# Attention and a Fourier mixer on one core: the query maximum subtracted on GpSimd, the exponential table loaded behind each root, and an empty step ahead of the transform's blocks

## The chip, the core and the metric

One core of a Trainium2 chip runs the whole kernel. Its engines work side by side, each in its own order of instructions: TensorE (PE: matmuls; PEld: its weight loads), VectorE (DVE), ScalarE (ACT), GpSimd (POOL); SyncE (SP) issues most transfers. The metric is the device time of one execution in microseconds, the median of several.

## The reference, cut to what matters

```python
# efficient attention, 8 batches, 8 heads, 576 tokens, head width 64
q_s = np.exp(q - max over the head's 64);   q_s = q_s / (sum over the 64 + 1e-9)
k_s = np.exp(k - max over the 576 tokens);  k_s = k_s / (sum over tokens + 1e-9)
kv  = einsum('bhsd,bhse->bhde', k_s, v)
x   = einsum('bhsd,bhde->bhse', q_s, kv)      # then heads side by side: (8, 576, 512)
# Fourier mixer and feed-forward
u  = x + real(fft(fft(x, tokens), columns))
un = (u - mean(u)) / sqrt(var(u) + 1e-6)
out = u + relu(un @ w_ch1) @ w_ch2            # 512 -> 2048 -> 512
```

All of it is in fp32.

## The kernel before

The rows are worked on in nine groups: the own tokens of the eight batches (four tiles of 128 rows each) and one group of tokens that the batches share. Group by group, TensorE does the up-projection and the down-projection (for the first group plainly, for the others by Strassen's seven products of halves). Into the up-projection of one group the attention of the next batch is mixed, step by step, and into the down-projection that batch's transform (the Fourier mixer) and its norm. A scheduler then orders the instructions of each engine by its own estimates, so a changed instruction can move others.

The query tiles. An even batch has five (four of its own and one of shared rows), an odd one four:

```python
def q_exp(self, it):
    q = self.live[it][0]
    heads = q.rearrange("p (h d) -> p h d", h=H)                       # 128 x 8 x 64
    V.reduce_max(m[:], heads, axis=AX.X, negate=True)                  # L519, DVE
    for h in range(H):
        nc.scalar.activation(heads[:, h, :], heads[:, h, :], ACT.Exp, bias=m[:, h:h + 1])   # L521, ACT
    V.reduce_sum(rec[:], heads, axis=AX.X)                             # L523
    V.tensor_scalar(out=rec[:], in0=rec[:], scalar1=ATT_EPS, ...)      # L524
    V.reciprocal(rec[:], rec[:])                                       # L525
    V.tensor_tensor(out=heads, in0=heads, in1=spread(rec), op=ALU.mult)  # L526
# then: four PE transposes (L532), ACT copy (L539; L545 for the shared rows), product with kv (L564)
```

The key tiles: maximum on DVE (L455), exponential with a bias on ACT (L457), PE transposes (L467), ACT copy (L468), product with v (L484), and the result scaled into place by DVE (`kvr`, L487).

The transform: four steps of folds on DVE and POOL (L603 to L625), then five blocks of PE products (L655, L658):

```python
    folds = [tokens_folded, columns_folded, by_frequency, columns_again] if b else [at_first]
    return folds + [lambda k=k: block(k) for k in (2, 3, 0, 1, 4)]
```

The norm of a group:

```python
def scales(s):
    nc.scalar.activation(std[:, s], mv[:, s, 1], ACT.Sqrt, bias=self.eps[:, 0:1])   # L730, ACT
    V.reciprocal(std[:, s], std[:, s])                                               # L731, DVE
    V.scalar_tensor_tensor(out=mv[:, s, 0], ...)                                     # L732, DVE
def normal(i):       # groups after the first
    nc.scalar.activation(un[:, 0:D], x, ACT.Identity, bias=..., scale=...)           # L744, ACT
def turn(i):         # four PE transposes (L750), one ACT copy (L754)
```

After it, DVE and POOL combine the transposed rows for Strassen (L348 to L351), and the next up-projection's matmuls (L850) start. In the up-projection, ACT takes the Relu (L857, L862) and POOL makes the sums of its results that the down-projection (L886) needs, four instructions at a time (`a_side`, L341 to L344). In the first group's down-projection (L789), the weights' Strassen sums are made and stored as well (L341 to L351 on DVE and POOL).

The exponential and the root are in different tables of ScalarE. A table load is put in front of an activation whose function is not in the loaded one.

Of the kernel before, what the change touches and what calls it, by code (L numbers as in the profile page):

```python
# [40 lines left out]
F32 = mybir.dt.float32  # L41
# [5 lines left out]
P = 128  # L47
# [75 lines left out]
class _Block:  # L123
# [389 lines left out]
    def q_exp(self, it):  # L513
        nc, V = self.nc, self.nc.vector
        q = self.live[it][0]
        heads = q.rearrange("p (h d) -> p h d", h=H)
        spread = lambda t: t[:].unsqueeze(2).to_broadcast([P, H, DH])
        m = self.small.tile([P, H], F32, tag="qm", name="qm", bufs=3)
        V.reduce_max(m[:], heads, axis=AX.X, negate=True)  # L519
        for h in range(H):  # L520
            nc.scalar.activation(heads[:, h, :], heads[:, h, :], ACT.Exp, bias=m[:, h:h + 1])  # L521
        rec = self.small.tile([P, H], F32, tag="qrec", name="qrec", bufs=3)
        V.reduce_sum(rec[:], heads, axis=AX.X)  # L523
        V.tensor_scalar(out=rec[:], in0=rec[:], scalar1=ATT_EPS, scalar2=None, op0=ALU.add)  # L524
        V.reciprocal(rec[:], rec[:])  # L525
        V.tensor_tensor(out=heads, in0=heads, in1=spread(rec), op=ALU.mult)  # L526
# [63 lines left out]
    def transform(self, b):  # L590


        nc, V, G = self.nc, self.nc.vector, self.nc.gpsimd
        Z = self.work.tile([P, KT, HD], F32, tag="Z", name="Z", bufs=1)
        self.Z[b] = Z
        x = {(c, u): self.xpart(b, c, u) for c in range(2) for u in range(2)}
        eo = {}

        def tokens_folded(some=range(4)):
            for i in some:  # L600
                e, op = ((V if b == 0 else G), ALU.add) if i < 2 else (V, ALU.subtract)
                eo[i] = self.halves()
                e.tensor_tensor(out=eo[i][:, 0:D], in0=x[i % 2, 0], in1=x[i % 2, 1], op=op)  # L603

        def columns_folded(some=range(4)):
            for i in some:
                e, op = ((V if b == 0 else G), ALU.add) if i < 2 else (V, ALU.subtract)
                t = eo[i]
                e.tensor_tensor(out=t[:, 1:HD], in0=t[:, 1:HD], in1=t[:, D - 1:HD:-1], op=op)
                if b == 0:  # L610
                    self.warm(t[:, 0:HD], 2)

        def by_frequency(some=range(4)):

            for i in some:
                e, op = ((G, ALU.add), (G, ALU.subtract), (V, ALU.add), (V, ALU.subtract))[i]
                one, two = eo[i // 2 * 2], eo[i // 2 * 2 + 1]
                (V if b == 0 else e).tensor_tensor(out=eo[i][:, NN:], in0=one[:, 0:NN], in1=two[:, 0:NN], op=op)

        def columns_again(some=(2, 3, 0, 1)):  # L620

            for i in some:
                t, y = eo[i], eo[i][:, NN:]
                V.tensor_tensor(out=t[:, 0:QD], in0=y[:, 0:QD], in1=y[:, HD:QD:-1], op=ALU.subtract)
                V.tensor_tensor(out=y[:, 0:QD], in0=y[:, 0:QD], in1=y[:, HD:QD:-1], op=ALU.add)  # L625

        def at_first():

            for some in ((2, 3), (0, 1)):
                for f in (tokens_folded, columns_folded, by_frequency, columns_again):  # L630
                    f(some)

            t = self.small.tile([P, 1], F32, tag="root", name="root", bufs=1)
            V.tensor_scalar(out=t[:], in0=eo[1][:, NN:NN + 1], scalar1=0.0, scalar2=None, op0=ALU.mult)
            nc.scalar.activation(t[:], t[:], ACT.Sqrt)
            self.wait_for(eo[1][:, NN:], [self.raws[i] for i in range(4)])

        def block(k):


            g = self.live["g", b]
            sines = k in (2, 3)
            own = slice(*{0: (NN, NN + QD), 4: (NN + QD, NN + QD + 1), 1: (0, QD), 2: (NN + 1, NN + QD + 1),
                          3: (1, QD)}[k])
            tail = slice(*{0: (0, QD), 4: (QD, QD + 1), 1: (NN, NN + QD), 2: (1, QD + 1), 3: (NN + 1, NN + QD)}[k])
            n = own.stop - own.start
            if k == KT:

                own, tail = slice(own.start, own.start + P), slice(tail.start, tail.start + P)
            full = self.acc((own.stop - own.start, 512))  # L650
            pz = full[0:n]
            f = sines * NM
            for odd, at, size in ((1, 0, MO), (0, MO, ME)):
                t = eo[3 - odd if sines else odd]
                nc.tensor.matmul(full[:, at:at + size], lhsT=t[:, own], rhs=self.ft[:, f + at:f + at + size], start=at == 0,  # L655
                                 stop=False, skip_group_check=True)
            f += 2 * NM
            nc.tensor.matmul(full[:, 0:NM], lhsT=g[:, tail], rhs=self.ft[:, f:f + NM], start=False, stop=True,  # L658
                             skip_group_check=True)
            z, zt = (self.Zr[0:1], self.ZTr[0:1]) if k == KT else (Z[0:n, k, :], self.ZT[0:n, k, :])  # L660
            nc.scalar.copy(paired(z), interleaved(pz[:, NT - 1:NT - 1 + 2 * ME])[:, 0:P, :])

            at = W * (b % 2)
            nc.scalar.mul(paired(zt[:, at:at + Q]), interleaved(pz[:, 0:2 * MO])[:, 0:NT - 1, ::-1],
                          -1.0 if sines else 1.0)
            nc.scalar.copy(paired(zt[:, at + Q:at + W]), interleaved(pz[:, 0:2 * ME])[:, NT - 2::-1, ::-1])

        folds = [tokens_folded, columns_folded, by_frequency, columns_again] if b else [at_first]
        return folds + [lambda k=k: block(k) for k in (2, 3, 0, 1, 4)]

    def second(self, z, zr, add):

# [43 lines left out]
    def norm(self, g):  # L716

        nc, V = self.nc, self.nc.vector
        mv = self.small.tile([P, 4, 2], F32, tag="mv", name="mv", bufs=2)
        std = self.small.tile([P, 4], F32, tag="std", name="std", bufs=2)  # L720
        unT = self.work.tile([P, 7, 2, HD], F32, tag="unT", name="unT", bufs=1)
        uns = {}

        def stats(i):
            st = self.small.tile([P, 6], F32, tag="st", name="st", bufs=2)
            V.bn_stats(st[:], self.xpart(g, i % 2, i // 2))
            V.bn_aggr(mv[:, i, :], st[:])

        def scales(s):
            nc.scalar.activation(std[:, s], mv[:, s, 1], ACT.Sqrt, bias=self.eps[:, 0:1])  # L730
            V.reciprocal(std[:, s], std[:, s])  # L731
            V.scalar_tensor_tensor(out=mv[:, s, 0], in0=mv[:, s, 0], scalar=-1.0, in1=std[:, s], op0=ALU.mult,  # L732
                                   op1=ALU.mult)

        def normal(i):
            un = self.halves()
            x = self.xpart(g, i % 2, i // 2)
            if g == 0:
                V.tensor_scalar(out=un[:, 0:D], in0=x, scalar1=std[:, i:i + 1], scalar2=mv[:, i, 0:1], op0=ALU.mult,
                                op1=ALU.add)  # L740
                if i == 1:
                    self.wait_for(un, [self.raws[i] for i in range(4, 11)])
            else:
                nc.scalar.activation(un[:, 0:D], x, ACT.Identity, bias=mv[:, i, 0:1], scale=std[:, i:i + 1])  # L744
            uns[i] = un

        def turn(i):
            pt = self.turned()
            for k in range(KT):
                nc.tensor.transpose(pt[:, k, :], uns[i][:, k * P:(k + 1) * P], self.ident[:])  # L750

            c, u = i % 2, i // 2
            cols = slice(c * P, (c + 1) * P)
            nc.scalar.copy(unT[:, u:u + 3:2, :, cols], pt[:].rearrange("p (a k) t -> p a k t", a=2))  # L754

        def all_stats():

            for some in ((0, 2), (1, 3)) if g == 0 else (range(4),):
                for i in some:
                    stats(i)  # L760
                scales(slice(some[0], 4, some[1] - some[0]))

        def combine():
            if g > 0:
                self.b_side(lambda i: unT[:, i], lambda i: unT[:, i], V, nc.gpsimd, V)

        return unT, [all_stats] + pipelined((0, 2, 1, 3), [normal, turn]) + [combine]
# [177 lines left out]
def kernel(ctx: ExitStack, tc: tile.TileContext, q, kT, v, w1, w2, ft,  # L945
# [4 lines left out]
    def front(b, loads=None):  # L950

        first = blk.attention(b, loads)
        steps = late(lambda: blk.transform(b), 9 if b else 6)
        mixes = [lambda c=c: blk.mix_own(b, c) for c in range(2)]
        if b % 2:

# [136 lines left out]
```

## Time and profile before

| | before |
|---|---|
| time, median of 3 (lowest to highest) | 1143.22 us (1142.0 to 1143.67) |
| span of the profiled execution | 1140.2 us |
| granted TensorE clock, mean | 0.996 |
| table loads in front of k's exponentials (L457) | 7, of 1283 ns each |
| table loads in front of the norm's root (L730) | 7, of 1283 ns each |
| query exponentials (L521) | 288, mean 337 ns |

The page gives each engine's busy time as a share of the span. The view by stretch splits that by time: for each stretch its length, the busy time of PE, PEld, DVE, ACT and POOL with the number of instructions in brackets, the granted clock, the share of DMA time and the GB/s. A timeline line gives start, duration, engine, source line, operation and shapes; in square brackets stands how long the engine had been idle before it, and what ended that.

### The profile page before, as it was taken

How to read it: one execution, taken by the hardware profiler on the slowest of the kernel's cores; microseconds unless marked ns; L12 is line 12 of the kernel's file. 1: busy time of each engine (PE TensorE's matmuls, PEld its weight loads, DVE VectorE, ACT ScalarE, POOL GpSimd, SP SyncE). 2: the span in 40 equal slices, each digit the busy share in tenths (PEclk: the TensorE clock that was granted, in tenths of full speed). 3: DMA queues.
4: the chain of work that ended last, by engine and by line, in shares of the span. 5: the costliest groups of instructions: out<-in, count | busy, mean ns of one | idle time of the engine just before them, and what ended most of it. 6: DMA issues, size and time to landing. Idle time of an engine off the chain costs nothing.

```text
span 1140.2 us, 14639 instructions
## 1 busy us (share of the span) xinstructions
PE 1098.6 (96%) x5472; PEld 919.1 (81%) x5472; DVE 543.4 (48%) x1110; ACT 397.7 (35%) x956; POOL 332.5 (29%) x302
## 2 busy tenths in 40 slices
PE   5899999989999999999999999999999999999997
PEld 4644556878888988888889888888889888888886
DVE  6785756488324833384435643683344352203201
ACT  6495423274124513371226322641233142201200
POOL 2075541245012600324024402260034213302320
PEclk9999999999999999999999999999999999999999
DMA  9377784463346534554356436543453344444451
GB/s 310 120 258 243 258 279 148 149 213 140 122 150 206 202 111 143 183 195 154 124 176 213 148 113 190 195 172 107 143 191 148 114 163 148 185 139 154 150 185 55
DMA packets 92549, 193.79 MB, mean 170 GB/s; under 512 B 23088, under 2 KB 59696, under 8 KB 85312
## 3 DMA queue, kind: packets, MB, share of 16 engines
q1 hardware_dynamic: 90680, 191.82, 49.5%
q10 hardware_dynamic: 1800, 1.05, 0.3%
q8 instruction: 43, 0.70, 0.2%
q14 instruction: 26, 0.21, 0.1%
HBM read 168.72 MB, written 28.31 MB: 173 GB/s over the span
## 4 chain that ended last, share of the span: by engine, by line
PE 79%; DVE 11%; ACT 4%; DMA 2%; issue 2%; POOL 1%; SPq 0%; ACTq 0%; POOLq 0%; DVEq 0%
PE bb L850 14%; PE bb L886 13%; PE bc L886 10%; PE bc L850 9%; PE ba L850 9%; PE ba L886 8%; PE acc L484 3%; PE acc L564 2%; PE bc L789 2%; PE acc L655 2%; PE acc L658 2%; PE acc L678 1%; PE tr L750 1%; PE tr L532 1%; PE tr L467 1%
## 5 line engine op out<-in xcount | busy, mean ns | idle before, releaser
L850 PE MATMUL bb<-unT,big 128*128 128x256 f32 x768 | 187.9, 381 | 0.3 <-DVE u L822 0.3
L886 PE MATMUL bb<-big 128*128 128x256 f32 x768 | 172.8, 379 | 0.0
L850 PEld LDWEIGHTS bb<-unT,big 128*128 128x128 f32 x768 | 142.8, 190 | 23.8 <-DVE u L818 3.4
L886 PEld LDWEIGHTS bb<-big 128*128 128x128 f32 x768 | 145.1, 190 | 20.1
L341 POOL TENSOR_TENSOR big<-big 128x512 f32<-128x512 f32 (+1 forms) x38 | 45.1, 1187 | 309.5 <-ACT big L862 305.6
L850 PE MATMUL bc<-unT,big 128*128 128x256 f32 x512 | 125.3, 379 | 0.0
L850 PE MATMUL ba<-unT,big 128*128 128x256 f32 x512 | 124.3, 379 | 0.0
L862 ACT ACTIVATE big<-big 128x512 f32<-128x512 f32 x96 | 60.2, 628 | 171.3 <-DVE big L861 171.0
L886 PE MATMUL bc<-big 128*128 128x256 f32 x512 | 116.5, 379 | 0.5 <-DVE x L903 0.5
L886 PE MATMUL ba<-big 128*128 128x256 f32 x512 | 114.1, 379 | 0.0
L886 PEld LDWEIGHTS bc<-big 128*128 128x128 f32 x512 | 95.9, 190 | 14.1 <-DVE x L903 0.9
L886 PEld LDWEIGHTS ba<-big 128*128 128x128 f32 x512 | 95.9, 190 | 12.3
L850 PEld LDWEIGHTS bc<-unT,big 128*128 128x128 f32 x512 | 95.5, 190 | 12.5
L850 PEld LDWEIGHTS ba<-unT,big 128*128 128x128 f32 x512 | 95.0, 190 | 11.7
L822 DVE TENSOR_TENSOR u<-bb,s 128x512 f32<-128x512 f32 x40 | 27.6, 689 | 134.8 <-PE bb L886 79.1
L521 ACT ACTIVATE q<-q,qm 128x64 f32<-128x64 f32 x240 | 61.5, 337 | 10.2 <-DVE qm L519 9.4
L349 POOL TENSOR_TENSOR unT<-unT 128x512 f32<-128x512 f32 x8 | 14.2, 1773 | 172.9 <-DVE unT L348 172.9
L818 DVE TENSOR_TENSOR u<-bb,s 128x512 f32<-128x512 f32 x40 | 27.6, 690 | 76.8 <-PE bb L850 38.1
L898 POOL TENSOR_TENSOR x<-x,u 128x512 f32<-128x512 f32 x14 | 17.7, 1267 | 148.2 <-DVE u L822 118.0
L861 DVE TENSOR_TENSOR big<-bc,u 128x512 f32<-128x512 f32 x64 | 44.1, 688 | 26.1 <-PE bc L850 25.3
L814 ACT COPY s<-ba 128x512 f32<-128x512 f32 x40 | 23.4, 584 | 89.4 <-PE ba L886 45.5
L754 ACT COPY unT<-tr 128x512 f32<-128x512 f32 x36 | 20.6, 585 | 86.5 <-PE tr L750 86.0
(221 smaller groups left out, 1656.7 us busy)
## 6 DMA issues: line engine op xcount, KB each, us to landing
big<-w1s SPq DMA_DIRECT2D x64, 896.0 KB
big<-w2s SPq DMA_DIRECT2D x56, 1024.0 KB
big<-in_w_dram SPq DMA_DIRECT2D x21, 512.0 KB
k<-in_kT_dram SPq DMA_DIRECT2D x26, 288.0 KB
q<-in_q_dram SPq DMA_DIRECT2D x27, 256.0 KB
v<-in_v_dram SPq DMA_DIRECT2D x26, 256.0 KB
words<-in_w_dram SPq DMA_DIRECT2D x11, 512.0 KB
w2s<-big SPq DMA_DIRECT2D x8, 512.0 KB
```

The costliest lines, as they stand in the source:

```text
L341: e1.tensor_tensor(out=to(4), in0=at(2), in1=at(3), op=ALU.add)
L484: nc.tensor.matmul(pk, lhsT=ks[:, c, :], rhs=v[:, c, :], start=(c == 0), stop=(c == NC - 1))
L521: nc.scalar.activation(heads[:, h, :], heads[:, h, :], ACT.Exp, bias=m[:, h:h + 1])
L564: nc.tensor.matmul(px[:, r * P:(r + 1) * P], lhsT=qT[:, r, :], rhs=self.kvr[b % 2][:, r, :], start=True, stop=True)
L655: nc.tensor.matmul(full[:, at:at + size], lhsT=t[:, own], rhs=self.ft[:, f + at:f + at + size], start=at == 0, stop=False, skip_group_chec ...
L814: nc.scalar.copy(temp("s1"), box["ba"][:])
L818: V.tensor_tensor(out=temp("u2"), in0=box["bb"][:], in1=box["s1"][:], op=ALU.add)
L822: V.tensor_tensor(out=temp("u3"), in0=box["bb"][:], in1=box["s1"][:], op=ALU.add)
L850: nc.tensor.matmul(bank()[:, i, :], lhsT=w[:, WA_AT[m], k * P:(k + 1) * P], rhs=unT[:, B_AT[m], k, :], start=first and i == 0 and k == 0, ...
L861: V.tensor_tensor(out=hp(i), in0=bank[:], in1=u[:], op=ALU.add)
L862: nc.scalar.activation(hp(i), hp(i), ACT.Relu)
L886: nc.tensor.matmul(bank()[:, i, :], lhsT=h[p][:, A_AT[m], i * P:(i + 1) * P], rhs=w[:, p, :], start=first and i == 0 and p == 0, stop=p == ...
```

## The change

Three things. The maximum of a query head is no longer given to eight exponentials as their bias: POOL subtracts it from the whole tile, and one exponential of 128 x 512 follows. For all norms but the first group's, a tiny exponential stands right behind the root, so that the table of exponentials is loaded there and not later in front of a key tile. From batch 2 on, the transform has an empty step between its folds and its blocks, so that the blocks are mixed one step later into the down-projection.

```diff
@@ q_exp
-        V.reduce_max(m[:], heads, axis=AX.X, negate=True)
-        for h in range(H):
-            nc.scalar.activation(heads[:, h, :], heads[:, h, :], ACT.Exp, bias=m[:, h:h + 1])
+        V.reduce_max(m[:], heads, axis=AX.X)
+        nc.gpsimd.tensor_tensor(out=heads, in0=heads, in1=spread(m), op=ALU.subtract)
+        nc.scalar.activation(q, q, ACT.Exp)
@@ transform
-        return folds + [lambda k=k: block(k) for k in (2, 3, 0, 1, 4)]
+        return folds + [lambda: None] * (b > 1) + [lambda k=k: block(k) for k in (2, 3, 0, 1, 4)]
@@ norm, scales
             nc.scalar.activation(std[:, s], mv[:, s, 1], ACT.Sqrt, bias=self.eps[:, 0:1])
+            if g > 0:
+                t = self.small.tile([P, 1], F32, tag="root", name="root", bufs=1)
+                nc.scalar.activation(t[:], std[:, 0:1], ACT.Exp)
             V.reciprocal(std[:, s], std[:, s])
@@ front: number of the transform's steps
-        steps = late(lambda: blk.transform(b), 9 if b else 6)
+        steps = late(lambda: blk.transform(b), (6, 9, 10)[min(b, 2)])
```

## The prediction

> **What bounds the kernel now.** I read the page's first two parts first, then the busy time by stretch, then the timeline around every place where TensorE (PE) stood still.
>
> ```profile
> span 1140.2 us, 14639 instructions
> PE 1098.6 (96%) x5472; PEld 919.1 (81%) x5472; DVE 543.4 (48%) x1110; ACT 397.7 (35%) x956; POOL 332.5 (29%) x302
> ```
>
> PE is the bound and its work does not change, so the change is worth only the PE idle time that it removes or adds. The busy time by stretch says where that idle is (first number after the length: PE busy):
>
> ```profile
> 0.00:60.00 60.00, 40.52 (x234) 33.75 (x234) 43.12 (x125) 35.11 (x100) 10.28 (x30) 0.97 0.65 205
> 120.00:150.00 30.00, 25.82 (x116) 15.77 (x115) 24.54 (x60) 15.60 (x49) 12.96 (x17) 1.00 0.82 296
> 150.00:220.00 70.00, 70.00 (x306) 47.19 (x305) 38.26 (x81) 20.70 (x47) 22.98 (x23) 1.00 0.56 179
> 220.00:260.00 40.00, 36.26 (x204) 30.74 (x203) 28.96 (x61) 26.41 (x74) 14.02 (x12) 1.00 0.58 199
> 260.00:460.00 200.00, 200.00 (x1054) 177.72 (x1054) 96.10 (x192) 64.54 (x165) 49.08 (x39) 1.00 0.44 152
> 460.00:500.00 40.00, 38.71 (x217) 33.62 (x216) 22.03 (x50) 21.96 (x55) 15.38 (x14) 1.00 0.66 225
> 700.00:760.00 60.00, 58.42 (x328) 51.16 (x327) 36.88 (x72) 31.97 (x82) 21.30 (x19) 1.00 0.58 199
> 1120.00:1140.20 20.20, 12.07 (x55) 9.97 (x53) 1.70 (x4) 0.00 (x0) 0.00 (x0) 0.88 0.18 51
> ```
>
> Start 19.5, batch 1's attention 4.2, batch 2's 3.7, batches 4 and 6 1.3 and 1.6, tail 8.1: 38 of the 41.6 us. Between, PE hardly rests. The tail is the last store, which the change leaves alone. So outside the start some 11 us can be had at all. A 128x256 matmul shows 379 ns but the next starts 216 ns later (32 in 6.91 us), so a stall is 0.16 us longer than the idle shown behind one. A steady stall looks like this, in batch 2's attention:
>
> ```profile
> 229.16 0.74 DVE L455 TENSOR_REDUCE km<-k 128x1 f32<-128x576 f32 x1
> 229.93 1.28 ACT L457 ACT_TABLE_LOAD   x1
> 231.22 0.78 ACT L457 ACTIVATE k<-k,km 128x576 f32<-128x576 f32 x1
> 232.14 0.66 PE L467 MATMUL tr<-ident,k 128*128 128x128 f32 x4 [1.47 <-ACT k L457]
> 236.79 4.88 ACT L521 ACTIVATE q<-q,qm 128x64 f32<-128x64 f32 x20
> 254.11 0.66 PE L532 MATMUL tr<-ident,q 128*128 128x128 f32 x4 [1.32 <-DVE q L526]
> ```
>
> The maximum of k is ready at 229.90, but the table load stands in front of its exponential, and PE waits 1.63 us in all. Further on ACT (ScalarE) is full of eights of small exponentials, and PE waits four more times for transposes of q: 0.77, 0.47 and 1.48 us.
>
> [...] Here the load takes 1283 ns, but the exponential starts 10 ns behind it: a switch is worth 1.28 us here[...]. [...] The trace has 337 ns for a 128x64 exponential with bias, eight of them in 2.02 us; a 128x512 Relu of SBUF without one takes 628. [...] The trace: 1.27 us for 128x512 undisturbed, against 0.69 on DVE (VectorE). [...] DVE's normalising product of q (L526) takes 0.69 at the median and up to 1.60, and its small addition (L524) 1.28 instead of 0.17 at 744.9, both while POOL works.
>
> **The change part by part.**
>
> *The query exponentials.* 36 tiles (five for an even batch, four for an odd one) each lose 2.02 us of ACT and gain 0.63 of ACT (as the 128x512 Relu) and 1.27 of POOL. ACT sheds 36 x 1.39 = 50 us, POOL gains 46 and goes from 29% to 33%. For one tile the chain hardly moves: 1.27 + 0.63 + about 0.1 of hand-over is 2.00 against 2.02. Only where tiles queue on ACT is anything gained.
> - Start: in 16.05 to 27.28 us four tiles' exponentials hold ACT for 8.2 us, mixed with copies. The POOL order puts three subtractions ahead of the folds of the shared rows and two behind them. ACT's order puts two exponentials ahead of the copy of the transposed shared rows, so that copy and the folds come about 1.1 us later. The last tile's exponential then ends near 25.3 instead of 27.28, after which DVE (three quarters busy) passes on most of it: PE's wait at 31.38 ends about 1.5 us earlier. **+1.5**.
> - Batch 1 (120 to 150 us): PE's 2.86 us wait at 123 is for data of k and stays. The one at 145.8 (1.65 us) is for DVE's eviction of kv, which stands in DVE's queue behind the sum of the fourth tile. That tile's subtraction now comes on POOL behind additions for the Strassen weights that wait for a DMA until 142.3. Subtraction to about 145.1, exponential to 145.8, against 144.3 now: the wait grows. **-1.0**.
> - Batch 2: the four-Strassen-sums of the up-projection (L341 to L344, 5.2 us) hold POOL until 235.2; the first maximum is there at 236.6, so the first tile is neither helped nor hurt, the later ones gain 1 to 2 us. Its table load also goes (below): 1.63 would fall by 1.28, but in the new PE order that transpose stands four matmuls (0.86 us) earlier, which eats most of it. Of the 4.3 us of listed waits I give back **+2.0**.
>
> *The table behind the root.* Loads go from 16 to 19: the seven in front of k's exponentials become one (batch 1, whose norm has no preload), each of eight norms gets one, and a second root load comes between the last two norms. Stalls that vanish: batches 4 and 6, at 476.9 and 720.5, each 1.20 us for the transpose and 0.35 for the product behind it; PE's order there has the transpose where it was. 2 x 1.55 = **+3.1**. The price is in the norm: the tiny exponential reads std, and the reciprocal overwrites std in place, so VectorE must wait for load and exponential, 1.28 + 0.20 us, before the normalised rows can be made. For groups 2 to 7 the transposes of the rows come 1.2 to 4 us behind the rows now, or are moved 1.7 to 3 us later, so this is hidden. For norm(1) at 191 to 201 us it is not: rows end 199.56, last transpose 200.18, next projection 200.62. **-1.5**.
>
> *The empty step.* For batches 2 on, most blocks of the transform come eight matmuls (1.73 us) later on PE, and so do most transposes of the norm in even groups. What waited there: 0.32 at 769.6 and 0.72 at 888.5 for the folds, 0.55 at 801.8 for the normalised rows. **+1.5**. The projection of the next group then follows the last transpose at once, as it does already at 446.7 without a stall (1.73 us of the first product go ahead of the one that needs the combined rows).
>
> Sum: 1.5 - 1.0 + 2.0 + 3.1 - 1.5 + 1.5 = 5.6 us, so 1143.2 - 5.6 = **1137.6 us**.
>
> **The rivals.**
> 1. *POOL becomes the wait.* [...] a subtraction behind four Strassen sums can be 5 us late, and a subtraction waiting for its maximum holds up sums that the down-projection needs. For it: 36 more POOL instructions[...]. Against: POOL now idles 306 us in front of L341, and in even batches the subtractions stand between finished groups of sums. It would cost 1 to 2 us in each of batches 2 to 6: 1143 to 1148.
> 2. *The gain at the start is larger.* If ACT alone held the start, 5 tiles x 1.39 = 7 us less work could become 4 to 5 us: 1133. Against: DVE does 2.4 us of work for each tile and is 79% busy from 20 to 40 us, and the folds of the shared rows get later.
> 3. *All is hidden:* the scheduler re-places transposes earlier wherever its estimate of ACT falls, and every place is again a near miss. Then 1142 to 1144.
> 4. *The norm's longer chain shows in every group*, 1 us x 6: it would cancel the table loads, 1142.
>
> **Range and chances.** The only large idle is at the start, and no step above moves more than 5 us, so 2% (23 us) is out of reach in both directions. The terms are each uncertain by 1 to 2 us, and eight new placements of PE work are not to be foreseen: 1131.5 to 1144.5. I give faster by over 2% 0.01, within 2% 0.98, slower by over 2% 0.01.
>
> **What would show it.** Right: ACT near 353 us busy (397.7 - 50 + 3 loads of 1.28 + 8 x 0.2), POOL near 378; no table load in front of k's exponentials after batch 1; no PE wait above 0.5 us near 470 to 480 and 715 to 725; a wait of 1 to 2 us near 201; first 60 us with 1 to 2 us less idle. Wrong: PE transposes of q waiting for POOL by way of ACT and DVE (rival 1), or more than 3 us won before 60 us (rival 2), or waits of PE for normalised rows in later groups (rival 4).

## The result and the profile after

| | before | after |
|---|---|---|
| time, median of 4 (lowest to highest) | 1142.61 us (1140.6 to 1143.67) | 1156.49 us (1154.42 to 1158.38) |
| ratio to before, 95% interval | | 1.0123 [1.01, 1.0146] |
| span of the profiled execution | 1140.2 us | 1155.1 us |
| granted TensorE clock, mean | 0.996 | 0.988 |

The change costs 1.2%, some 14 us, where the prediction had a gain of 5.6. First the page's head of the kernel after:

```profile
span 1155.1 us, 14453 instructions
PE 1106.3 (96%) x5472; PEld 925.6 (80%) x5472; DVE 545.3 (47%) x1110; ACT 357.6 (31%) x715; POOL 371.4 (32%) x338
```

The work moved as foreseen: ACT from 397.7 to 357.6 (predicted 353), POOL from 332.5 to 371.4 (predicted 378). PE has the same 5472 matmuls, yet is 7.7 us longer busy: part of them ran at a lower clock. So the loss is in PE's waits and in its clock. The busy time by stretch of the kernel after (length, then PE, PEld, DVE, ACT, POOL busy, clock, DMA share, GB/s):

```profile
0.00:60.00 60.00, 39.98 (x219) 34.08 (x220) 40.82 (x113) 26.65 (x61) 14.43 (x34) 0.91 0.65 204
...
260.00:460.00 200.00, 196.61 (x1037) 174.47 (x1036) 97.74 (x199) 60.07 (x128) 62.52 (x51) 0.99 0.45 156
460.00:500.00 40.00, 39.38 (x214) 34.35 (x213) 17.77 (x38) 12.11 (x22) 13.21 (x12) 1.00 0.55 181
500.00:700.00 200.00, 197.50 (x1054) 175.80 (x1053) 102.46 (x205) 63.43 (x132) 64.35 (x53) 1.00 0.47 160
```

From 460 to 500 there is a little less idle, as predicted. But 260 to 460, where PE did not rest before (200.00), now has 3.4 us of idle, 500 to 700 has 2.5, and the clock of the first 60 us fell from 0.97 to 0.91. As the kernels drift apart, a fixed window compares different work. So I cut the two traces at PE's own marks: the start of the first matmul of each up- and each down-projection. In us, worked out from the starts in the traces:

| from mark to mark | before | after | difference | predicted (minus is a gain) |
|---|---|---|---|---|
| start, to the first up-projection | 61.0 | 64.7 | +3.7 | -1.5 |
| first up-projection | 56.2 | 57.0 | +0.8 | 0 |
| first down-projection (batch 1's attention, norm(1)) | 83.4 | 88.3 | +4.9 | +1.0 + 1.5 |
| up-projection with batch 2 | 67.9 | 71.5 | +3.6 | -2.0 |
| up-projections with batches 4 and 6 | 131.3 | 135.0 | +3.8 | -3.1 |
| up-projections with batches 3, 5, 7 | 187.1 | 187.8 | +0.7 | 0 |
| down-projections with batches 2 to 7 (transforms, norms) | 348.9 | 346.8 | -2.2 | -1.5 |
| the rest, to PE's last matmul | 196.8 | 196.8 | 0 | 0 |

The loss lies in the rows in which queries are worked on; the down-projections with the transforms got faster. The waits of PE in the kernel after, by what they waited for (us in total, times, longest), show a releaser that was 0.3 us in all before:

```profile
PE bb L855 <- DVE u L823: 5.0, 2, 2.5
PE bb L855 <- DVE u L827: 2.6, 1, 2.6
```

These are three waits of an up-projection's matmul for `u`, DVE's eviction of an earlier product. The timeline of the second of them:

```profile
508.26 0.68 DVE L519 TENSOR_REDUCE qm<-q 128x8 f32<-128x512 f32 x1
...
508.95 1.71 POOL L341 TENSOR_TENSOR big<-big 128x512 f32<-128x512 f32 x1 [4.29 <-DVE qm L519]
...
510.61 1.04 POOL L520 TENSOR_TENSOR q<-q,qm 128x512 f32<-128x512 f32 x1
...
511.69 0.63 ACT L521 ACTIVATE q<-q 128x512 f32<-128x512 f32 x1 [1.85 <-POOL q L520]
...
512.35 0.69 DVE L523 TENSOR_REDUCE qrec<-q 128x8 f32<-128x512 f32 x1 [2.75 <-ACT q L521]
...
513.07 1.08 DVE L524 TENSOR_SCALAR qrec<-qrec 128x8 f32<-128x8 f32 x1
...
514.42 1.59 DVE L526 TENSOR_TENSOR q<-q,qrec 128x512 f32<-128x512 f32 x1
515.93 0.68 DVE L823 TENSOR_TENSOR u<-bb,s 128x512 f32<-128x512 f32 x1
...
516.67 1.78 PE L855 MATMUL bb<-unT,big 128*128 128x256 f32 x7 [2.50 <-DVE u L823]
```

The maximum is ready at 508.94. POOL has just begun one of the sums for the down-projection, in front of the subtraction in its queue: 1.7 us. (The releaser named at that sum is not its own: its input, a Relu of ACT, ended at 508.87, and the maximum happened to end just after.) The subtraction takes 1.04, the exponential 0.63. Meanwhile DVE stands idle for 2.75 us, because the sum of this tile is next in its queue, and the eviction `u` that PE needs stands behind the tile's sum, addition and product. Two of those are stretched while POOL works (1.08 for an addition that takes 0.17 elsewhere, 1.59 for a product that takes 0.69). Of 36 subtractions, 31 started within 0.6 us of their maximum. The five that came later are two of batch 1 (1.2 and 1.7 us) and the first tiles of batches 3, 5 and 7 (3.0, 1.7, 1.7), and right behind these three stand the waits at 270.6, 513.8 and 758.6, of 2.79, 2.66 and 2.66 us.

Then the clock. The third of those waits, in PE's busy time by stretch of the kernel after (PE alone, then clock, DMA share, GB/s):

```profile
757.90:761.50 3.60, 1.12 (x7) 1.00 0.36 101
...
761.90:765.30 3.40, 3.40 (x10) 0.50 0.00 0
765.30:768.70 3.40, 3.40 (x21) 1.00 0.02 5
```

After the wait PE runs 3.4 us at half clock: the first eight matmuls take 3.43 us, where the eight behind the equal wait at 513.8 take 1.99. Over the stretch some 1.6 us are lost on top. The wait at 513.8 was followed by no such stretch (clock 1.00 in the 3.4 us behind it). Before, there was one at 49.9 and one in the tail; after, there are six ahead of the tail (at 17.8 of double length, 34.9, 65.6, 154.3, 273.8, 761.9). Adding up over all PE instructions by how much the time from start to start exceeds the median of that shape gives 44.5 us before and 59.7 after, of which 1.6 and 10.6 are half clock: of the loss of 15 us in this execution some 8 to 9 are clock, the rest longer waits. That share is not fixed: the other three executions of the kernel after were granted 0.989 to 0.994, and the one at 0.994 still took 1154.42 us. What brings a stretch on is not shown: of the three waits of 2.79, 2.66 and 2.66 us for `u`, those at 270.6 and 758.6 were followed by one (at 273.8 and 761.9) and the one at 513.8 was not.

At the start the order of DVE's queue has changed. DVE and POOL of the kernel after, then PE:

```profile
26.53 0.69 DVE L523 TENSOR_REDUCE qrec<-big 128x8 f32<-128x512 f32 x1
27.14 0.68 DVE L519 TENSOR_REDUCE qm<-big 128x8 f32<-128x512 f32 x1
...
27.89 1.04 POOL L520 TENSOR_TENSOR big<-big,qm 128x512 f32<-128x512 f32 x1 [4.11 <-DVE qrec L524]
...
34.09 3.10 PE L564 MATMUL acc<-kvr,qT 128*128 128x128 f32 x16 [1.21 <-ACT xs L581]
```

And the same maximum and the same matmuls before:

```profile
21.13 0.67 DVE L519 TENSOR_REDUCE qm<-big 128x8 f32<-128x512 f32 x1
...
31.38 2.05 PE L564 MATMUL acc<-kvr,qT 128*128 128x128 f32 x16 [1.21 <-ACT xs L581]
```

The maximum of the last own tile now stands behind other tiles' sums and products, 6 us later. PE's wait ends 2.7 us later instead of 1.5 earlier, and its 16 matmuls run into a half-clock stretch (3.10 against 2.05). In batch 1 it is alike: the maximum of the fourth tile ends at 149.21 (before at 139.41, in a down-projection that began 4.5 us earlier), and at the head of ACT's queue its exponential waits for it and the subtraction, with the copy of another, already transposed tile behind it:

```profile
150.46 0.63 ACT L521 ACTIVATE spare<-spare 128x512 f32<-128x512 f32 x1 [4.81 <-POOL spare L520]
151.11 0.59 ACT L539 COPY qT<-tr 128x512 f32<-128x512 f32 x1
```

That transpose was done at 148.34. PE waits 1.85 us for the copy.

Of the experiments that follow, one disturbed execution of e5 (1295.04 us, clock 0.85) and one of e9 (1628.34 us, 0.67) are left out, and as the former is the one that was profiled, no wait of e5 is read.

### The profile page after: what moved, and what is told of

Its sections match the earlier page's. It is cut to its first block, busy times and chain, and to the rows that moved or that the text cites. A ratio compares the mean times of both kernels' runs of the same rounds, so it can differ in the third digit from the quotient of the medians.

```text
span 1155.1 us, 14453 instructions
## 1 busy us (share of the span) xinstructions
PE 1106.3 (96%) x5472; PEld 925.6 (80%) x5472; DVE 545.3 (47%) x1110; ACT 357.6 (31%) x715; POOL 371.4 (32%) x338
## 4 chain that ended last, share of the span: by engine, by line
PE 72%; DVE 2%; POOL 1%; ACT 0%; issue 0%; POOLq 0%; DVEq 0%; ACTq 0%
PE bb L891 14%; PE bb L855 12%; PE bc L891 10%; PE ba L891 10%; PE bc L855 8%; PE ba L855 8%; PE acc L484 2%; PE acc L655 1%; PE acc L658 1%; PE acc L564 1%; PE acc L679 1%; PE tr L755 1%; PE tr L467 1%; PE tr L532 1%; PE acc L580 0%; PE acc L574 0%
## 5 line engine op out<-in xcount | busy, mean ns | idle before, releaser
L855 PE MATMUL bb<-unT,big 128*128 128x256 f32 x768 | 190.4, 385 | 7.6 <-DVE u L823 5.0
L341 POOL TENSOR_TENSOR big<-big 128x512 f32<-128x512 f32 (+1 forms) x38 | 46.2, 1216 | 257.6 <-ACT big L867 244.1
L855 PEld LDWEIGHTS ba<-unT,big 128*128 128x128 f32 x512 | 95.3, 191 | 11.9
L342 POOL TENSOR_TENSOR big<-big 128x512 f32<-128x512 f32 (+1 forms) x38 | 47.9, 1261 | 1.9
L520 POOL TENSOR_TENSOR q<-q,qm 128x512 f32<-128x512 f32 x30 | 31.8, 1076 | 43.1 <-DVE qm L519 29.2
```

What stands on the lines that cost most here:

```text
L341: e1.tensor_tensor(out=to(4), in0=at(2), in1=at(3), op=ALU.add)
L342: e1.tensor_tensor(out=to(2), in0=at(0), in1=at(2), op=ALU.subtract)
L520: nc.gpsimd.tensor_tensor(out=heads, in0=heads, in1=spread(m), op=ALU.subtract)
L855: nc.tensor.matmul(bank()[:, i, :], lhsT=w[:, WA_AT[m], k * P:(k + 1) * P], rhs=unT[:, B_AT[m], k, :], start=first and i == 0 and k == 0, ...
```

## The experiments

All times are medians; the kernel before, measured beside them, was at 1142.82 us for e1 to e4, 1143.03 for e5 to e8, 1143.48 for e9 to e12 and 1143.47 for e13 and e14. Ratios are to that.

**Each part alone, and the two without GpSimd.** Part A is the subtraction with the single exponential, B the table behind the root, C the empty step. The edits are the parts of the diff above.

> The kernel before with the subtraction on POOL and one exponential alone; no table load behind the root, no empty step. Theory P (the subtraction is the loss: [...]the late exponential holds the sum at the head of DVE's queue, and the eviction of a Strassen bank behind it comes late): 1154 to 1161 us, with PE waits of over 2 us for u (the banks' evictions) in the attention of batches 2, 4 and 6 and a start about 4 us longer. Theory N (the longer chain of the norm and the shifted blocks are the loss): 1138 to 1143.

> The kernel before with the table load behind the root alone. Theory P: 1138 to 1142 us (the table stalls near 476 and 720, 1.2 to 1.55 us each, go; 1 to 1.5 us are lost at norm(1) near 200). Theory N: 1148 or more.

> The kernel before with the empty step alone. Theory P: 1140 to 1143 us (the waits for folds, 0.3 to 0.7 us each, go). Theory N: 1146 or more.

> The kernel after with the eight biased exponentials put back (table load behind the root and empty step stay). Theory P: 1137 to 1141 us, faster than the kernel before and about 17 us faster than the one after. Theory N: about 1156, as the one after. If the three parts do not add up (this far from the sum of the two single parts), the scheduler's new order decides, not the parts.

| | us | ratio, 95% interval |
|---|---|---|
| e1, A alone | 1154.99 | 1.011 [1.0092, 1.0128] |
| e2, B alone | 1141.13 | 0.9986 [0.9972, 1.0] |
| e3, C alone | 1141.88 | 1.0001 [0.9992, 1.001] |
| e4, B and C | 1140.66 | 0.9979 [0.9971, 0.9988] |

The loss is part A. B alone shows 1.7 us by the medians, at the edge of its interval. B and C together gain 2.2 us; the norm's longer chain does not turn that into a loss.

**The single exponential without GpSimd.** The maximum of the whole row is given as bias. (The quotient stays what the reference defines except for the 1e-9 in the denominator and for heads whose maximum lies so far below the row's that their exponentials underflow.)

```diff
-        V.reduce_max(m[:], heads, axis=AX.X, negate=True)
-        for h in range(H):
-            nc.scalar.activation(heads[:, h, :], heads[:, h, :], ACT.Exp, bias=m[:, h:h + 1])
+        V.reduce_max(row[:], q, axis=AX.X, negate=True)
+        nc.scalar.activation(q, q, ACT.Exp, bias=row[:, 0:1])
```

> The kernel before with the maximum of a whole row (one for all eight heads) as the bias of one 128x512 exponential: no POOL work, no eights. It leaves out the maximum by head; the softmax of each head is the same but for rounding. Theory Q (POOL itself is the loss: its queue, its speed[...]): 1136 to 1142 us, and a start like that of the kernel before (PE's wait for the copy of shared rows ends near 31.4 us). Theory O (the order: with short exponentials the scheduler puts sums and products of earlier tiles on VectorE ahead of the maxima of later ones, so the later tiles start late): the maxima of the start's last two tiles at about 22 and 27 us and not at 18 and 21, the wait ends near 33 to 34, and the time is 1145 to 1153.

1142.45 us, ratio 0.9992 [0.9985, 0.9999]. ScalarE's shorter work alone neither costs nor brings anything to speak of. So the order that the scheduler makes of short exponentials, by itself, is not the loss.

**The subtraction on VectorE**, `nc.gpsimd.tensor_tensor` replaced by `nc.vector.tensor_tensor`, nothing else:

> The kernel before with the subtraction on VectorE in place of POOL, and one exponential. Theory Q: near the kernel before, 1140 to 1146 us (0.69 us more of VectorE for each of 36 tiles). Theory O: about as the POOL form alone, 1150 to 1158.

1150.65 us, ratio 1.0063 [1.0048, 1.0078], so over 7 of the 12 us are there with no GpSimd in it. Here VectorE gets 36 instructions more (1146 instead of 1110, 561.5 us busy instead of 543.4), and PE waits for it: 1.2 to 1.5 us each for `u` near 267, 509 and 755 and for the transform's folds near 406 and 652, and 4.6 us near 126 for the data of k (2.86 before). A subtraction of a whole tile between maximum and exponential hurts on either engine.

**Where GpSimd's subtraction hurts.** The new form for batch 0 only (e7, `if it[1] == 0`, else the eight), and for batches 1 to 7 only (e8):

> The kernel before with the POOL subtraction in batch 0 alone (the start), eights in the others. Both theories: the part of the loss that lies in the start, 1145 to 1149 us if the parts add up (the POOL form alone is at 1155, before at 1142.8; the first up-projection started 3.5 us later there, and up to 2 us of half clock came behind it).

> The kernel before with the POOL subtraction in batches 1 to 7, eights in batch 0. If the parts add up: 1149 to 1152 us, with the waits near 150 (1 to 3 us), 269 (3 us), 412 and 657 (1.3 us each) as in the POOL form alone.

1144.98 us (1.0016 [1.0007, 1.0024]) and 1151.27 us (1.0076 [1.0059, 1.0093]): about 2 and 8 us over the kernel before, 10 of e1's 12. The start is not the main seat of the loss.

**The link and the load, each alone.** Both take the row's maximum as bias (e5's form). In e9 it goes through GpSimd as a copy of 128 x 1; in e10 GpSimd makes two subtractions of 128 x 256 per tile into a tile that nobody reads (and `row` has six buffers in place of three).

```diff
 e9
         V.reduce_max(row[:], q, axis=AX.X, negate=True)
+        nc.gpsimd.tensor_copy(link[:], row[:])
-        nc.scalar.activation(q, q, ACT.Exp, bias=row[:, 0:1])
+        nc.scalar.activation(q, q, ACT.Exp, bias=link[:, 0:1])
 e10
         V.reduce_max(row[:], q, axis=AX.X, negate=True)
+        for _ in range(2):
+            nc.gpsimd.tensor_tensor(out=apart, in0=ident, in1=spread(row), op=ALU.subtract)    # 128x256
         nc.scalar.activation(q, q, ACT.Exp, bias=row[:, 0:1])
```

> The row's maximum is the bias of one 128x512 exponential, but it passes through GpSimd first, as a copy of 128x1: the exponential hangs on GpSimd's queue, and GpSimd has almost no work from it. Theory D (what costs is that each query tile waits in GpSimd's queue behind sums of the down-projection, and that a waiting copy holds up those sums): 1146 to 1152 us, with TensorE waits of 1 to 3 us behind the up-projection's results near 265 and 510. Theory L (what costs is GpSimd's 1 us of work per tile and that VectorE is slowed beside it): 1141 to 1144, as with the row's maximum alone (1142.5).

> The row's maximum is the bias of one 128x512 exponential, and GpSimd makes two subtractions of 128x256 per tile into a tile that nobody reads: its work is there and hangs on the maximum, but nothing waits for it. Theory D: 1141 to 1145 us, since no query tile waits for GpSimd. Theory L: 1147 to 1153, nearly all of the 12 us that the subtraction alone cost, with VectorE's small addition behind the query's sum near 1 us instead of 0.17. If neither this nor the copy costs more than 3 us, it is the 1 us added between maximum and exponential with what the scheduler makes of it.

| | us | ratio, 95% interval |
|---|---|---|
| e9, link | 1150.35 | 1.0059 [1.0037, 1.0081] |
| e10, load | 1147.95 | 1.004 [1.0031, 1.0049] |

Neither theory has it alone: over the kernel before the link costs 6.9 us and the load 4.5. That their sum is near e1's 12 is not an account of it, since the places differ. By PE's marks the link loses 3.1 us at the start, 3.1 in the first down-projection and 2.8 in the later ones, the load 5.3 in the first down-projection and otherwise nothing on balance; in the up-projection with batch 2, where e1 loses 4.2, both gain (0.8 and 1.6). Nor is e10 the load alone. Its subtractions take 1.35 us per tile against 1.08 in the kernel after, and they too wait in GpSimd's queue for the maximum: 2.86 us in front of those at 387.85, with the transform's first fold behind them. What VectorE loses beside GpSimd does not explain the load: its small addition takes 334 ns on average in e10, 347 in the kernel before and 239 in the kernel after. PE waits 3.3 us near 146.6 for `kvr`, with 6.8 us at half clock from about its end on; the eviction stands in VectorE's queue behind sums of query tiles and of Strassen weights, and VectorE is busy for 11.9 us of the 12 from 138 to 150.

**The same link on VectorE**, to tell GpSimd's queue from the new order that any link brings:

```diff
-        nc.gpsimd.tensor_copy(link[:], row[:])
+        nc.vector.tensor_copy(link[:], row[:])
```

> As the run with the copy of the row's maximum on GpSimd, but VectorE makes the copy: the extra link is there, GpSimd's queue is not in it. If it is GpSimd's queue that cost 8 us there: 1141 to 1144 us. If any further instruction between maximum and exponential costs as much, because the scheduler then orders the engines differently: 1147 to 1151.

1139.77 us, ratio 0.997 [0.9958, 0.9981]. The link as such costs nothing; through GpSimd it costs 10.6 us more (some 8 if e5, which has no link, is the measure). The timeline of the link on GpSimd (e9) at the first tile of batch 3:

```profile
259.20 0.66 DVE L519 TENSOR_REDUCE qrow<-q 128x1 f32<-128x512 f32 x1
...
260.50 1.73 POOL L343 TENSOR_TENSOR big<-big 128x512 f32<-128x512 f32 x1
...
262.31 1.27 POOL L344 TENSOR_TENSOR big<-big 128x512 f32<-128x512 f32 x1
...
263.52 0.18 POOL L521 COPY qlink<-qrow 128x1 f32<-128x1 f32 x1
263.74 0.72 ACT L522 ACTIVATE q<-q,qlink 128x512 f32<-128x512 f32 x1 [3.48 <-POOL qlink L521]
...
268.19 1.13 PE L851 MATMUL bb<-unT,big 128*128 128x256 f32 x4 [1.19 <-DVE u L823]
```

And on VectorE (e13):

```profile
255.46 0.69 DVE L519 TENSOR_REDUCE qrow<-q 128x1 f32<-128x512 f32 x1 [1.85 <-DMA q<-in_q_dram]
...
256.18 0.15 DVE L521 COPY qlink<-qrow 128x1 f32<-128x1 f32 x1
...
256.37 1.51 ACT L522 ACTIVATE q<-q,qlink 128x512 f32<-128x512 f32 x2 [0.69 <-DVE qlink L521]
...
259.15 1.04 PE L851 MATMUL bb<-unT,big 128*128 128x256 f32 x4
```

On GpSimd a copy of 0.18 us starts 3.66 us after the maximum, behind two sums of the down-projection, and PE waits for `u`; on VectorE it starts at once and PE goes on. But this copy is the only one of e9's 36 that started over 0.7 us late. The rest lies elsewhere. The two profiled executions are 12.2 us apart, and by PE's marks 2.6 us of that come up to the first up-projection, 1.2 and 3.0 in the first group's two projections, 2.3 with batch 2, and 1.8 in each of two later down-projections, where PE waits 1.7 us near 406 and 651 for folds that do not wait in e13. In front of the first of these GpSimd's queue does what theory D also says: a copy that waits for its maximum holds up work that has its data.

```profile
389.76 0.58 POOL L521 COPY qlink<-qrow 128x1 f32<-128x1 f32 x1 [4.24 <-DVE qrow L519]
390.30 1.27 POOL L604 TENSOR_TENSOR eo<-x 128x512 f32<-128x512 f32 x1
```

The fold L604 needs the first three copies of `x` at most (in e13 it starts ahead of the fourth). The third ended at 383.04, and the fold starts 7.3 us later, with GpSimd idle for 4.2 of them; near 635 it is the same. Whether that is what PE then waits for is not shown: the second fold stands in e9 behind a sum (L341) that waits for ScalarE, and in e13 ahead of it. The queues of GpSimd and VectorE have another order at all these places; that a cross-engine link makes the scheduler choose a worse one is an inference from that, and not separately tried.

**Maximum and subtraction earlier in the program.** They stand with the query's load, one step ahead of the exponential; A alone otherwise. The edit leaves both out for the four own tiles of batch 0, which are loaded earlier and by another path: 32 subtractions run, not 36, and those four exponentials are taken of the queries as they are.

> Subtraction on GpSimd alone, but maximum and subtraction stand with the query's load in the program, one step ahead of the exponential, so that they come early in the queues of VectorE and GpSimd. If the loss is the place of maximum and subtraction in the queues (late maxima, products at the head of VectorE's queue): 1142 to 1147 us instead of 1155, with no wait of 3 us near 266 to 270. If it is GpSimd's work and its hold on VectorE: 1149 to 1155. If waiting for loads blocks VectorE or GpSimd: above 1155.

1150.42 us, ratio 1.0059 [1.0044, 1.0074]: 4.6 us of e1's 12 come back, the other 7 do not. But by PE's marks 3.0 us of what comes back lie ahead of the first up-projection, where the four tiles without subtraction are, so that part says nothing of the place in the queues. Near 266 the wait is 1.7 us instead of 3.0, and near 147 it is 3.7. The place in the program is at most some 3 us of the loss; for the first tile of batch 3 it changed little in the queue, as its subtraction still starts 3.4 us behind its maximum.

**How the parts meet.** A and B without C:

> Subtraction on GpSimd and table behind the root, without the empty step. If the three parts simply add up, 12.2 - 1.5 over the kernel before: 1153.5 us. If the new waits of 2.7 us at 513.8 and 758.6 in the changed kernel come from the table's new place (the query's exponentials then come earlier in the batch than they can be fed), they are here as well: 1155 to 1158. If they come from the empty step: none of them, 1152 to 1154.

1159.09 us, ratio 1.0132 [1.0113, 1.0152], the slowest of all. The waits of 2.7 us for `u` at 513.4 and 761.0 are there; in e1 they are not, though e1 waits 1.3 us for folds near 412 and 657, which the changed kernel does not. So by the medians B, which shows a gain alone, makes A worse by some 3 us, though the intervals of e1 and e11 overlap. The folds' waits are in e11 too (1.3 us near 412 and 659), so it is C that takes them away.

**All of it without GpSimd.** e5's form with B and C:

> The row's maximum as bias of one 128x512 exponential, with the table behind the root and the empty step: all that the change was for, but with no work for GpSimd. If the parts add up: 1143 - 0.9 - 2.4 = 1140 us, level with the table and the step alone (1140.7). If ScalarE's freed 50 us open up more once the table loads are gone: 1137 to 1139.

1138.94 us, ratio 0.9961 [0.9947, 0.9975]. This is the lowest median of the study, 0.4% under the kernel before; the intervals of e4 (0.9979 [0.9971, 0.9988]) and e13 overlap with it. Its page's head:

```profile
span 1135.5 us, 14401 instructions
PE 1096.9 (97%) x5472; PEld 919.0 (81%) x5472; DVE 541.6 (48%) x1110; ACT 359.1 (32%) x715; POOL 334.9 (29%) x302
```

ACT is where the change wanted it, and POOL where it was before. By PE's marks: -0.7 at the start, -1.0 in the first up-projection, +2.8 in the first down-projection, -1.1 with batch 2, -3.2 with batches 4 and 6, +0.7 with 3, 5 and 7, -2.2 in the later down-projections, together -4.7. At the start the last maximum is late here too, but its exponential follows at once:

```profile
25.17 0.68 DVE L519 TENSOR_REDUCE qrow<-big 128x1 f32<-128x512 f32 x1
25.88 0.72 ACT L520 ACTIVATE big<-big,qrow 128x512 f32<-128x512 f32 x1 [1.26 <-DVE qrow L519]
```

## Why the prediction was wrong

The prediction summed six terms of PE's waits, with one assumption under three of them: that a subtraction on GpSimd only replaces time on ScalarE ("For one tile the chain hardly moves"). For most tiles that holds: at the median the exponential starts 1.53 us after the maximum's end, 1.04 of it the subtraction, and is one of 0.63; before, the first of the eight started after 1.04. The step that failed is the one built on it, "Only where tiles queue on ACT is anything gained", with no loss elsewhere: one slow tile is enough, and what waits is not only the tile.

- *Start, +1.5.* Measured -3.7. The failing step is "The last tile's exponential then ends near 25.3 instead of 27.28": it kept DVE's order of before, and that exponential ended at 29.59. The new order put the last maximum 6 us later, and the subtraction with its hand-overs came on top. The late maximum alone is not a loss: in e12, without the subtraction, it comes 4 us later than before, yet the exponential ends at 26.60 and PE's wait at 30.72, 0.7 us earlier than before. In e7, where only this batch has the subtraction, the loss is 2 us.
- *Batch 1, -1.0, and norm(1), -1.5.* Sum -2.5, measured -4.9. Both were right in sign, the first not in its mechanism: the wait for `kvr` that was to grow stayed (1.65 and 1.60), and one of 1.85 for the copy of a transposed tile came ahead of it, because the maximum of the fourth tile came 5 us later against PE's marks. The waits of batch 1 grew from 2.86 and 1.65 to 2.97, 1.85 and 1.60, 1.9 us more, and the two waits at the norm are 0.40 and 0.70 against 0.26, 0.8 more. The term that was missing is the half-clock stretch at 154.3, 1.6 us.
- *Batch 2, +2.0.* The listed waits fell from 4.35 to 3.54 us, a gain of 0.8. The loss came behind them: 2.79 us at 270.6 for `u` and the half clock after it, and the row of the table is +3.6. "The later ones gain" was said of the tiles of batch 2; the first tile of batch 3 stood in the same stretch, behind L343 and L344.
- *Table behind the root, +3.1.* The mechanism was right: one load is left in front of k's exponentials, in batch 1. The size was half: at 490.7 and 735.5 the transposes no longer wait, but the product behind them waits 0.78 us for its copy in place of 0.35, so 2 x 0.77 = 1.5. Alone it shows 1.7 (e2). Together with the subtraction it brought the waits at 513.8 and 758.6 (e11).
- *Empty step, +1.5.* The waits of 0.32, 0.72 and 0.55 are gone, and the folds' waits that the subtraction alone brings (1.3 twice in e1) as well. The later down-projections are 2.2 us shorter. Alone the step shows no gain that its interval separates from none (e3), though B and C together have one.
- *The rivals.* Rival 1 happened: a subtraction behind the Strassen sums, PE waiting by way of ACT and DVE. It was put aside with "POOL now idles 306 us in front of L341", which is an average; the first tiles of batches 3, 5 and 7 meet those sums all the same. Its other half, a subtraction that waits for its maximum and holds up work behind it, is seen as well, at the folds (e9), without a price of its own. The rival's price of 1 to 2 us in each of five batches was placed wrongly too: 2.7 us in three places, some 1.6 for the clock behind a wait, and the start. Rival 4 fell (e4); rivals 2 and 3 fell with the start and the sign.

The range of 13 us assumed that the terms err independently. They did not: nearly all of them hung on the same GpSimd subtraction. With that left out and the single exponential kept (e12), 4.5 us are gained by the medians, close to the sum of 5.6, and most terms are near too: 0.7 at the start (1.5 predicted), 1.1 with batch 2 (2.0), 3.2 with batches 4 and 6 (3.1), 2.2 in the later down-projections (1.5). That the first down-projection agrees (-2.8 against -2.5) is in part luck, since 1.0 of it was worked out from the subtraction on GpSimd.

What stays open: of the 10.6 us between e9 and e13 only the wait near 267 is followed from GpSimd's queue to PE instruction by instruction; at the folds the hold-up is seen, its effect on PE is not shown. And since each edit makes the scheduler order all engines anew, differences of 2 to 3 us between variants (e5 and e13, say, where VectorE's copy adds work and the time falls by 2.7) may be luck of the order; I build nothing on them.

## What to carry to other kernels

Moving work from one engine to another that is idle on average adds a link to a chain: look at what stands in front of it in the new engine's queue at each place, and at what stands behind the waiting consumer in the old one, since work that has nothing to do with the delay can come late as well (here DVE stood idle for 2.75 us with the eviction `u` behind the waiting sum, and PE waited 2.66 us for `u`). In a kernel whose matmul engine is 96% busy, price a new wait at its length plus a possible half-clock stretch (here two of three waits of 2.7 to 2.8 us had one behind them, of 3.4 us and a cost of some 1.6). If an operation can be made cheaper on the engine where it is (here one bias for the row instead of eight), try that ahead of moving it.

## What the runs showed of the hardware

Ahead of the tail of the kernel after, the half-clock stretches of TensorE (granted clock 0.50) lasted 3.4 us each, the one at 17.8 twice that; the one at 761.9 cost some 1.6 us and followed a wait of 2.66 us, in a kernel whose PE is 96% busy. The same wait 245 us earlier was followed by none, and neither was one of 3.5 us near 127 in e9 (clock 1.00 from 120 to 150). GpSimd's in-place subtraction of a 128x512 tile with a maximum spread over 64 columns took 1.04 us undisturbed (mean 1.08), less than its 1.27 for two full operands that the prediction had used. And a copy of 128 elements took 0.18 us on GpSimd undisturbed and 0.15 on VectorE, so the 10.6 us between e9 and e13 come from where it stands and not from what it takes.
